# Eleven products instead of twelve for w_in from block 3 on, g as one tile, and Strassen's sums 512 wide

## The chip, the cores and the metric

The kernel runs on one NeuronCore of a Trainium2 chip. The metric is the time of one execution on the device in microseconds. Before the change it is 675.13 us, the median of three runs (674.52 to 676.1).

## The reference

A linear-attention recurrence (the delta rule) for 4 sequences, 8 heads, 768 steps and a head size of 48, in float32, feeds a two-layer network on 3072 tokens:

```python
for t in range(S):
    y[t]  = q[t] @ state
    v_old = state.T @ k_n[t]                      # k_n: k over its norm
    state = state + beta[t] * outer(k_n[t], v[t] - v_old)
x = y.transpose(...).reshape(3072, 384)           # 4*768 tokens, 8 heads * 48
h = x @ w_in                                      # w_in: 384 x 2048
g = h * clip(h + 3, 0, 6) / 6
out = g @ w_out                                   # w_out: 2048 x 384
```

The weights arrive as float64 and are converted in the kernel.

## The kernel before

**The recurrence in chunks.** The 768 steps are cut into 24 chunks of 32, and 4 sequences times 32 steps fill the 128 partitions. In chunk t the function `chain` multiplies the state with the chunk's keys and queries (`ks`, L798), forms R from v and that (L892 twice, then L898, on VectorE), multiplies R with X, a triangular inverse (`pz`, L819), copies the result to Z on ScalarE (L916), updates the state (`su`, L927 and L945), and gives the output y (`py`, `yt`), which lands transposed in `xT`. `prep` makes the chunk's normalised keys kb on GpSimd (L502), transposes keys and queries (`pt`, L516), and forms the triangular matrices (`sc`, L539 and L550); `mask` (L478) and `scaled` (L490) prepare the masks mb and the keys times beta, bkb, on GpSimd.

**The inverse.** Chunk 0 is a group by itself, and then four chunks make a group (chunks 1 to 4, 5 to 8, 9 to 12 and so on). `inverse(g)` computes X for a whole group on VectorE: a transposition (L461), 60 small elimination steps that depend on each other (L751 multiplies, L756 subtracts), a memset (L760) and a transposition into X (L465). The first chunk of the group needs X at its `pz`.

**The network in blocks.** Two chunks make a block of 256 tokens, so there are 12 blocks. The first layer of a block takes the 2048 columns of w_in in 16 pieces of 128 (`up`, L983: for each piece three products of 128x128 with 256 tokens, then Relu on ScalarE, L991, and minimum times h on VectorE, L994, into `g`). From block `UF = 5` on, `up_by_eleven` takes two pieces together: a Strassen scheme with eleven products of 128x128x128 instead of twelve, with sums of weights made once in `weight_sums` (on GpSimd, L1020, during the second layer of block `UF - 1`, some of them in w_in in place), sums of tokens made once per block in `token_sums` (VectorE, L1046), and sums inside PSUM and g: a copy on ScalarE (L1069), two additions on GpSimd (`plus_minus`, L1020), two on VectorE (L1084, L1088), a copy and a Relu on ScalarE (L1091; L1095, which writes r into the buffer of `o`) and the last step on VectorE (L1098). `T1x`, `T2x`, `T4x` lie in unused columns of `beta_tok`.

The second layer is plain for blocks 0 and 1 (`down`, L1145). From block 2 on `down_by_seven` makes seven half-size products (L1210, in two halves each) in Strassen-Winograd's way. Four sums of quarters of g are formed in place on VectorE (L1196, the function `sums`, `lo` and `hi` halves), each by four instructions that take two pieces of 128 columns. Results are copied by ScalarE (L1217), added on GpSimd or VectorE (L1220) and written out by SyncE's queue (`to_dram`, L1134).

**The order.** Every engine works in the order in which the kernel is written down; nothing is rescheduled. The first chunks follow a list written by hand (`ORDER`). From chunk 5 on a loop places, for each chunk, 15 units. In each unit it takes steps of the chain and the preparation, one unit of the network (`mlp_units`: the first layer of a block has 16, the second by seven 14 to 15) and a number of elimination steps of the next group's inverse (`fill`). How many is worked out from the room that VectorE is taken to have in this unit:

```python
USED = {"up": 0.42, "eleven": 1.0, "down": 0.8}
...
room = max(1.65 - USED[mode["of"]] - CHAIN.get(u, 0), 0.15) / mode["mean"]
due += room * left / max((GS - i) * NU - u, 1)
```

`mode["of"]` says which kind of layer runs, `mode["mean"]` is 0.72 up to the last plain first layer and 0.4 after. So `UF` and `USED` move the elimination steps too. For group 3 (chunks 9 to 12) the steps begin in chunk 7; for the later groups they begin in the second chunk of the group before.

**PSUM.** Four buffers with the tag `pm` serve ph, pt, pz, py, yt and po in turn; two with the tag `pc` serve ks, su and sc.

**The tile g.** g is allocated as eight tiles of two pieces each, [128, 2, 256], from a pool with eight buffers.

Of the kernel before, what the change touches and what calls it, by code (L numbers as in the profile page):

```python
# [9 lines left out]
FP32 = mybir.dt.float32  # L10
# [36 lines left out]
def kernel(  # L47
# [21 lines left out]
    nc = tc.nc  # L69
# [3 lines left out]
    P = B * C  # L73
# [6 lines left out]
    NFC = FF // 128  # L80
    assert NKT * 128 == DM == H * D and NFC * 128 == FF
    CB = 2
    TB = CB * P
# [121 lines left out]
    for j, value in enumerate((1.0, -1.0)):  # L205
        m = mask2[:, j, :]
        for b in range(B):
            nc.gpsimd.memset(mask2[rows(b), j, :], value)
            nc.gpsimd.affine_select(
                out=mask2[rows(b), j, :], in_=mask2[rows(b), j, :], pattern=[[1, C]],  # L210
# [96 lines left out]
    for i, n in enumerate((0, 1, 2, 3, 4, 5, 0, 1, 3, 4, 5, 0, 1, 5, 0, 1)):  # L307
        s, f = weights[i][0].shape[1:]
# [49 lines left out]
    def convert():  # L358

        needs("beta")  # L360
        for i in range(NW):
            needs(("raw", i))
            if weights[i][1].dtype != FP32:
                d = raws[i]
                hi, lo = d[:, :, :, 1], d[:, :, :, 0]
                m = spare[:, 2, WP * NKT : 2 * WP * NKT].bitcast(U32).rearrange(
                    "p (s f) -> p s f", s=d.shape[1]
                )
                mf = m.bitcast(FP32)
                nc.vector.tensor_scalar(  # L370
                    out=m, in0=hi, scalar1=0x000FFFFF, scalar2=0x00100000,
                    op0=ALU.bitwise_and, op1=ALU.bitwise_or,
                )
                yield
                nc.vector.scalar_tensor_tensor(  # L375
                    out=mf, in0=lo, scalar=2.0**-32, in1=m, op0=ALU.mult, op1=ALU.add
                )
                past.add(("seen", i, 1))
                yield
                needs(("scale", i))  # L380
                nc.vector.scalar_tensor_tensor(
                    out=weights[i][0], in0=mf, scalar=2.0**-20, in1=like(es[i % 2], i).bitcast(BF16),
                    op0=ALU.mult, op1=ALU.mult,
                )
            past.add(("w", i))
            yield
# [570 lines left out]
    gs, pos, evicts = {}, {}, []  # L957
# [13 lines left out]
    def up(blk, half_of=None):  # L971

        cols = slice(0, TB) if half_of is None else slice(half_of * P, half_of * P + P)
        name = "u" if half_of is None else "ab"[half_of]
        needs(*(("seam", blk * CB + i) for i in range(CB) if half_of in (None, i)))
        xT = xTs[blk]
        for f in range(NFC):
            needs(("w", f * 128 // WP))
            key = ("ph", blk, f, half_of)
            ring("pm", NPM, key)  # L980
            ph = psM.tile([128, TB], FP32, name="ph", tag="pm")
            for s in range(NKT):
                nc.tensor.matmul(  # L983
                    ph[:, cols], lhsT=w_in[:, s, f * 128 : (f + 1) * 128], rhs=xT[:, s, cols],
                    start=(s == 0), stop=(s == NKT - 1),
                )
            if f % 2 == 0 and not half_of:
                gs[blk, f // 2] = mlp.tile([128, 2, TB], FP32, name="g", bufs=NFC // 2)

            def first(f=f, g=gs[blk, f // 2][:, f % 2, cols], ph=ph[:, cols], key=key):  # L990
                nc.scalar.activation(out=g, in_=ph, func=ACTF.Relu, bias=half, scale=1.0 / 6.0)  # L991

                def rest():
                    nc.vector.scalar_tensor_tensor(  # L994
                        out=g, in0=g, scalar=1.0, in1=ph, op0=ALU.min, op1=ALU.mult
                    )
                    read(key)
                    if half_of is not None:
                        past.add(("g", half_of, f))

                pending[name].append(rest)

            relus[name].append(first)
            if f == NFC - 1 and not half_of == 0:
                past.add(("up", blk))
            yield

    UF = 5
    S1, S2, S4 = (sums_in[:, i] for i in range(3))

    def w_tiles(s, i):
# [37 lines left out]
    def up_by_eleven(blk):  # L1049
        needs(("sums", blk))  # L1050
        B11, T3x, B21, B22, B31, B32 = x_tiles(blk)
        phs, ready = {}, {}

        def mm(ph, n, w, x, start=False, stop=False):
            nc.tensor.matmul(  # L1055
                ph[:, n], lhsT=w, rhs=x, start=start, stop=stop, skip_group_check=True
            )

        def begin(j):
            key = ("ph", blk, "by", j)  # L1060
            ring("pm", NPM, key)
            ph = phs[j] = psM.tile([128, 4, P], FP32, name="ph", tag="pm")
            mm(ph, 0, W11[:, j], B11, start=True)
            mm(ph, 1, S1[:, j], T1x)
            mm(ph, 2, W21[:, j], T3x)
            mm(ph, 3, S2[:, j], T2x)
            gs[blk, j] = mlp.tile([128, 2, TB], FP32, name="g", bufs=NFC // 2)
            gt = gs[blk, j][:].rearrange("p i (t c) -> p (i t) c", c=P)
            nc.scalar.activation(out=gt, in_=ph[:], func=ACTF.Copy)  # L1069
            plus_minus(gt[:, 3:1:-1], gt[:, 0:2], gt[:, 3:1:-1], ALU.add)  # L1070
            plus_minus(gt[:, 0], gt[:, 0], gt[:, 2], ALU.add)

        def end(j):
            ph = phs.pop(j)
            mm(ph, 0, W12[:, j], B21)
            mm(ph, 1, S4[:, j], B22)
            mm(ph, 2, W22[:, j], T4x)
            mm(ph, 0, W13[:, j], B31)
            mm(ph, 1, W13[:, j], B32)
            mm(ph, 2, W23[:, j], B31)  # L1080
            mm(ph, 3, W23[:, j], B32, stop=True)
            g = gs[blk, j][:].rearrange("p i c -> p (i c)")
            gt = gs[blk, j][:].rearrange("p i (t c) -> p (i t) c", c=P)
            nc.vector.tensor_tensor(  # L1084
                out=gt[:, 1:3], in0=ph[:, 1:3],
                in1=gt[:, 3].unsqueeze(1).to_broadcast([128, 2, P]), op=ALU.add,
            )
            nc.vector.tensor_tensor(out=gt[:, 3], in0=ph[:, 3], in1=gt[:, 0], op=ALU.add)  # L1088

            def first():  # L1090
                nc.scalar.activation(out=gt[:, 0], in_=ph[:, 0], func=ACTF.Copy)  # L1091
                read(("ph", blk, "by", j))
                ro = mlp.tile([128, CB, DM], FP32, name="o", bufs=1)
                r = ro[:].rearrange("p c m -> p (c m)")[:, 0 : 2 * TB]
                nc.scalar.activation(out=r, in_=g, func=ACTF.Relu, bias=half, scale=1.0 / 6.0)  # L1095

                def rest():
                    nc.vector.scalar_tensor_tensor(  # L1098
                        out=g, in0=r, scalar=1.0, in1=g, op0=ALU.min, op1=ALU.mult
                    )  # L1100

                ready[j] = rest

            ready[j] = first
            if j == NPR - 1:
                past.add(("up", blk))

        def go(j):
            if j in ready:
                ready.pop(j)()  # L1110

        begin(0)
        yield
        begin(1)
        yield
        for j in range(NPR):
            end(j)
            go(j - 1)
            if j + 2 < NPR:
                yield  # L1120
                begin(j + 2)
                go(j)
                yield
            else:
                go(j)
                if j == NPR - 1:
                    go(j)
                yield
# [47 lines left out]
    def quarters():  # L1176

        for o, a, b in ((T1, B12, B11), (T2, B22, T1), (T4, T2, B21)):
            for f in range(0, HF, 2):
                nc.vector.tensor_tensor(  # L1180
                    out=o[:, f : f + 2], in0=a[:, f : f + 2], in1=b[:, f : f + 2], op=ALU.subtract
                )
                yield
# [4 lines left out]
        )  # L1188

    def down_by_seven(blk):  # L1190
        def A(f, i, j):
            return gs[blk, (f + HF * j) // 2][:, :, i * P : i * P + P]

        def sums(op, out, a, b, fs):
            for f in fs:
                nc.vector.tensor_tensor(out=A(f, *out), in0=A(f, *a), in1=A(f, *b), op=op)  # L1196

        lo, hi, A11, A12, A21, A22 = (0, 2), (4, 6), (0, 0), (0, 1), (1, 0), (1, 1)
        o = mlp.tile([128, CB, DM], FP32, name="o", bufs=1)
        u = mlp.tile([128, HM], FP32, name="u", bufs=1)[:]  # L1200
        C11, C12, C21, C22 = (o[:, c, m : m + HM] for c in range(CB) for m in (0, HM))
# [115 lines left out]
    def chained(*gens):  # L1317
        for gen in gens:
            yield from gen
# [64 lines left out]
        return norms(g, i, size(g) if g > 1 else 2 if t == 2 else 1)  # L1384

    mlp = ctx.enter_context(tc.tile_pool(name="mlp", bufs=2))
    rest = chained(convert(), quarters())
    gens.update(
        a=scales(), c=rest, w=pieces(), q=queries(), v=values(), B=betas(), k=keys(), z=settings(), s=more_settings(),
# [26 lines left out]
    with tc.manual_schedule():  # L1416
# [10 lines left out]
        fill = inverse_of(2)  # L1427
        loads = iter(())
        left = due = 0
        USED = {"up": 0.42, "eleven": 1.0, "down": 0.8}  # L1430
        CHAIN = {0: 0.45, 1: 0.75, 2: 0.75, 3: 0.4, 4: 0.4, 6: 0.5, 9: 0.8, 10: 0.6, 14: 0.2}
        for t in range(LS, N):
            g, i = group(t)
# [92 lines left out]
```

## Time and profile before

| | |
|---|---|
| time, median of three runs | 675.13 us |
| span of the profiled execution, first to last instruction | 673.6 us |
| median less span | 1.5 us |
| PE busy | 636.8 us, 95% |
| VectorE (DVE) busy | 497.2 us, 74% |
| ScalarE (ACT) busy | 271.2 us, 40% |
| GpSimd (POOL) busy | 206.4 us, 31% |
| mean granted clock of TensorE | 0.992 |

No time is given for the profiled execution beside its span; so the span is used with the 1.5 us that the median lies above it. In the profile, PE is TensorE's matmul and PEld its weight load, which overlaps; a float32 matmul of the program stands as two instructions. The slices are fortieths of the span, 16.8 us each. A group's idle time is the engine's wait in front of the group, with what ended it. The chain that ended last is followed back from the end, and where it leaves TensorE, TensorE need not have been idle: it may have had other work until just before.

In the stretch from 189 to 631 us a block takes two stages of about 25 us: the first layer of a block (with an even chunk's start in it) and its second layer (with the odd chunk's). Block 3's first layer runs from 238.27 to 265.10, block 4's from 289.79 to 316.62, and the eleven-products blocks 5, 6 and 7 from 340.93, 391.08 and 441.19. Chunk 7 starts (with `ks`) at 216.6, chunk 8 at 242.2, chunk 9 at 267.7, chunk 12 at 344.3, chunk 13 at 369.4.

### The profile page before, as it was taken

What the parts mean: (1) busy time and instruction counts of PE and PEld (TensorE: products, weight loads), DVE (VectorE), ACT (ScalarE), POOL (GpSimd) and SP (SyncE); (2) the same over time, 40 slices, a digit from 0 to 9 for tenths busy, and PEclk for the clock granted to TensorE, in tenths of its full rate; (3) what the DMA queues carried; (4) which work ended last, traced back from release to release, by engine and by line L of the source; (5) the groups of instructions that cost most, each with busy time, mean ns of one, the idle gap of its engine ahead of it and who ended that gap; (6) DMA issues with size and microseconds to landing.
All of it is one profiled execution on the core that took longest, in us unless ns stands there. A gap on an engine that the chain in (4) does not pass through costs nothing.

```text
span 673.6 us, 26871 instructions
## 1 busy us (share of the span) xinstructions
PE 636.8 (95%) x11768; PEld 578.6 (86%) x11768; DVE 497.2 (74%) x1226; ACT 271.2 (40%) x532; POOL 206.4 (31%) x320
## 2 busy tenths in 40 slices
PE   2667989999999999999999999999999999999997
PEld 2557877776688988988999999999999999999997
DVE  5978876888545678947888957988748988557354
ACT  5995777422143232232235235245244144153250
POOL 6230231102431031254155255055042141232330
PEclk9989899999999999999999999999999999999999
DMA  7995336402041030032030030020020020010000
GB/s 192 243 218 131 91 78 150 84 1 48 15 82 28 2 72 2 3 70 39 3 64 12 2 67 9 3 61 3 2 49 3 2 49 2 17 23 2 26 1 23
DMA packets 88500, 33.29 MB, mean 49 GB/s; under 512 B 80160, under 2 KB 83232, under 8 KB 88384
## 3 DMA queue, kind: packets, MB, share of 16 engines
q1 hardware_dynamic: 88128, 31.29, 20.9%
q8 instruction: 92, 1.51, 0.9%
q10 hardware_dynamic: 256, 0.30, 0.2%
q14 instruction: 24, 0.20, 0.1%
HBM read 26.84 MB, written 4.72 MB: 47 GB/s over the span
## 4 chain that ended last, share of the span: by engine, by line
PE 86%; DVE 6%; DMA 2%; ACT 2%; issue 2%; SPq 1%; POOL 0%; ACTq 0%; DVEq 0%; POOLq 0%
PE po L1210 27%; PE ph L1055 20%; PE ph L983 15%; PE po L1145 6%; PE ks L798 3%; PE pz L819 3%; PE su L927 3%; PE py L819 3%; PE sc L539 3%; PE pt L516 3%; ACT spare L348 1%; PE yt L864 1%; DVE spare L375 1%; DMA spare<-in_moe_w_in_dram 1%; DMA qb<-in_q_dram 1%
## 5 line engine op out<-in xcount | busy, mean ns | idle before, releaser
L1055 PE MATMUL ph<-xT,w_in 128*128 128x128 f32 x784 | 122.9, 278 | 0.0
L983 PE MATMUL ph<-xT,w_in 128*128 128x256 f32 (+1 forms) x576 | 114.9, 350 | 3.4 <-DVE g L994 2.1
L1210 PE MATMUL po<-w_out,g 128*128 128x192 f32 x640 | 110.6, 326 | 0.0
L983 PEld LDWEIGHTS ph<-xT,w_in 128*128 128x128 f32 x576 | 94.3, 192 | 15.3 <-DVE g L994 2.5
L1055 PEld LDWEIGHTS ph<-xT,w_in 128*128 128x128 f32 x784 | 103.9, 192 | 1.4 <-ACT KQ L524 0.2
L1210 PEld LDWEIGHTS po<-w_out,g 128*128 128x128 f32 x640 | 104.1, 190 | 0.2
L1020 POOL TENSOR_TENSOR g<-g 128x256 f32<-128x256 f32 x112 | 68.1, 610 | 83.9 <-ACT g L1069 79.5
L1210 PE MATMUL po<-spare,g 128*128 128x192 f32 x480 | 86.7, 332 | 0.0
L1210 PEld LDWEIGHTS po<-spare,g 128*128 128x128 f32 x480 | 77.2, 190 | 1.8
L991 ACT ACTIVATE g<-ph,halves 128x256 f32<-128x256 f32 (+1 forms) x96 | 41.2, 436 | 79.1 <-PE ph L983 79.1
L1220 POOL TENSOR_TENSOR o<-o,u 128x192 f32<-128x192 f32 x18 | 15.0, 835 | 172.1 <-ACT o L1217 97.4
L1196 DVE TENSOR_TENSOR g<-g 128x256 f32<-128x256 f32 x160 | 63.4, 443 | 3.4 <-PE po L1210 3.1
L1069 ACT ACTIVATE g<-ph 128x512 f32<-128x512 f32 x56 | 33.4, 596 | 79.9 <-PE ph L1055 76.7
L756 DVE TENSOR_TENSOR A<-A,pr 128x30 f32<-128x30 f32 (+9 forms) x150 | 59.0, 393 | 3.7
L751 DVE TENSOR_TENSOR pr<-A 128x30 f32<-128x30 f32 (+9 forms) x150 | 55.2, 368 | 2.7
L994 DVE SCALAR_TENSOR_TENSOR g<-g,ph 128x256 f32<-128x256 f32 (+1 forms) x96 | 35.0, 370 | 26.0 <-ACT g L991 25.7
L348 ACT ACTIVATE spare<-spare,places 128x768 uint16<-128x768 uint16 (+1 forms) x56 | 52.4, 940 | 2.0 <-DMA spare<-in_moe_w_in_dram 1.1
L1084 DVE TENSOR_TENSOR g<-ph,g 128x256 f32<-128x256 f32 x56 | 23.4, 419 | 38.1 <-PE ph L1055 24.1
L1217 ACT ACTIVATE o<-po 128x192 f32<-128x192 f32 x40 | 13.2, 330 | 82.5 <-PE po L1210 78.9
L1098 DVE SCALAR_TENSOR_TENSOR g<-o,g 128x512 f32<-128x512 f32 x56 | 40.8, 729 | 7.3 <-ACT o L1095 7.3
L1145 PE MATMUL po<-w_out,g 128*128 128x384 f32 x128 | 45.6, 493 | 0.0
L1095 ACT ACTIVATE o<-g,halves 128x512 f32<-128x512 f32 x56 | 40.5, 722 | 11.3 <-DVE g L1098 5.7
(141 smaller groups left out, 991.4 us busy)
## 6 DMA issues: line engine op xcount, KB each, us to landing
kf<-in_k_dram SPq DMA_DIRECT2D x96, 48.0 KB, 2.8
qb<-in_q_dram SPq DMA_DIRECT2D x96, 48.0 KB, 2.9
vf<-in_v_dram SPq DMA_DIRECT2D x96, 48.0 KB, 2.1
out_dram<-o SPq DMA_DIRECT2D x92, 48.0 KB, 1.6
spare<-in_moe_w_in_dram SPq DMA_DIRECT2D x4, 768.0 KB, 6.7
w_out<-in_moe_w_in_dram SPq DMA_DIRECT2D x4, 768.0 KB, 6.0
w_out<-in_moe_w_out_dram SPq DMA_DIRECT2D x4, 768.0 KB, 6.0
spare<-in_moe_w_out_dram SPq DMA_DIRECT2D x4, 768.0 KB, 4.6
```

The source lines that it names most:

```text
L348: nc.scalar.activation(out=z, in_=z if n else d.bitcast(I16)[:, :, :, 3], func=func, bias=places[:, n : n + 1], scale=scale,)
L751: nc.vector.tensor_tensor(out=pv, in0=A[:, j + 1 :, j].unsqueeze(2).to_broadcast([n, w, j]), in1=A[:, j, 0:j].unsqueeze(1).to_broadcast([n ...
L756: nc.vector.tensor_tensor(out=A[:, j + 1 :, 0:j], in0=A[:, j + 1 :, 0:j], in1=pv, op=ALU.subtract)
L983: nc.tensor.matmul(ph[:, cols], lhsT=w_in[:, s, f * 128 : (f + 1) * 128], rhs=xT[:, s, cols], start=(s == 0), stop=(s == NKT - 1),)
L991: nc.scalar.activation(out=g, in_=ph, func=ACTF.Relu, bias=half, scale=1.0 / 6.0)
L1020: nc.gpsimd.tensor_tensor(out=out, in0=a, in1=b, op=op)
L1055: nc.tensor.matmul(ph[:, n], lhsT=w, rhs=x, start=start, stop=stop, skip_group_check=True)
L1095: nc.scalar.activation(out=r, in_=g, func=ACTF.Relu, bias=half, scale=1.0 / 6.0)
L1098: nc.vector.scalar_tensor_tensor(out=g, in0=r, scalar=1.0, in1=g, op0=ALU.min, op1=ALU.mult)
L1145: nc.tensor.matmul(pos[c][:], lhsT=gs[blk, f // 2][:, f % 2, c * P : (c + 1) * P], rhs=w_out[:, f, :], start=(f == 0), stop=(f == NFC - 1),)
L1196: nc.vector.tensor_tensor(out=A(f, *out), in0=A(f, *a), in1=A(f, *b), op=op)
L1210: nc.tensor.matmul(ps[n][:], lhsT=A(f - f % 2, *a)[:, f % 2], rhs=b[:, f], start=(f == 0), stop=(f == HF - 1),)
```

## The change

`UF` becomes 3: blocks 3 and 4 also use `up_by_eleven`, and `weight_sums` runs beside block 2's second layer. g becomes one tile, `g_all`, of [128, 16, 256], allocated once for all blocks; the functions take slices of it. With that, a Strassen sum takes four pieces in one instruction (128 partitions, 4 x 128 columns) where it took two, so each of the four sums has two instructions and not four. `USED["down"]` becomes 0.7.

```diff
-            if f % 2 == 0 and not half_of:
-                gs[blk, f // 2] = mlp.tile([128, 2, TB], FP32, name="g", bufs=NFC // 2)
+            gs[blk, f // 2] = g_all[:, f - f % 2 : f - f % 2 + 2]
...
-    UF = 5
+    UF = 3
...
-            gs[blk, j] = mlp.tile([128, 2, TB], FP32, name="g", bufs=NFC // 2)
-            gt = gs[blk, j][:].rearrange("p i (t c) -> p (i t) c", c=P)
+            gs[blk, j] = g_all[:, 2 * j : 2 * j + 2]
+            gt = gs[blk, j].rearrange("p i (t c) -> p (i t) c", c=P)
...
-        def A(f, i, j):
-            return gs[blk, (f + HF * j) // 2][:, :, i * P : i * P + P]
-
-        def sums(op, out, a, b, fs):
-            for f in fs:
-                nc.vector.tensor_tensor(out=A(f, *out), in0=A(f, *a), in1=A(f, *b), op=op)
-
-        lo, hi, A11, A12, A21, A22 = (0, 2), (4, 6), (0, 0), (0, 1), (1, 0), (1, 1)
+        def A(f, i, j, n=2):
+            return g_all[:, f + HF * j : f + HF * j + n, i * P : i * P + P]
+
+        def sums(op, out, a, b, f):
+            nc.vector.tensor_tensor(out=A(f, *out, 4), in0=A(f, *a, 4), in1=A(f, *b, 4), op=op)
+
+        lo, hi, A11, A12, A21, A22 = 0, 4, (0, 0), (0, 1), (1, 0), (1, 1)
...
+    g_all = mlp.tile([128, NFC, TB], FP32, name="g", bufs=1)
...
-        USED = {"up": 0.42, "eleven": 1.0, "down": 0.8}
+        USED = {"up": 0.42, "eleven": 1.0, "down": 0.7}
```

## Prediction

> **What bounds the kernel now.** I read the page first (busy shares, slices), then the table by stage, then the chain that ended last, then VectorE's timeline at two seams.
>
> ```profile
> PE 636.8 (95%) x11768; PEld 578.6 (86%) x11768; DVE 497.2 (74%) x1226; ACT 271.2 (40%) x532; POOL 206.4 (31%) x320
> PE   2667989999999999999999999999999999999997
> DVE  5978876888545678947888957988748988557354
> ```
>
> TensorE is full from about 105 us to the end, so past the start only two things change the time: TensorE work, and moments when TensorE waits. The stages show what a block's first layer costs (columns: length, busy time and instructions of PE, PEld, DVE, ACT, POOL, then clock, DMA share, GB/s):
>
> ```profile
> 238.27:265.10 26.83, 26.83 (x429) 23.03 (x428) 23.78 (x60) 9.56 (x20) 6.45 (x9) 1.00 0.23 46
> 289.79:316.62 26.83, 26.83 (x429) 23.04 (x428) 16.34 (x40) 9.56 (x20) 15.47 (x23) 1.00 0.36 69
> 340.93:366.77 25.84, 25.84 (x509) 25.15 (x508) 22.98 (x52) 12.93 (x26) 14.43 (x23) 1.00 0.24 49
> 391.08:416.88 25.80, 25.80 (x508) 25.11 (x508) 16.54 (x39) 12.93 (x26) 13.58 (x23) 1.00 0.24 49
> ```
>
> The first two rows are blocks 3 and 4 by plain products, the others blocks 5 and 6 by eleven; the recurrence's pieces between the products are the same. The third thing to see is a seam (start, length, what), where the inverse for chunks 9 to 12 ends and `pz` of chunk 9 needs it:
>
> ```profile
> 267.70 1.08 PE ks L798 x64
> ...
> 273.24 1.99 DVE X L465
> 275.23 0.14 issue
> 275.37 0.88 PE pz L819 x63
> ```
>
> From the start of `ks`, TensorE has other work for 7.37 us (1.08 + 1.51 + 0.44 + 1.30 + 0.44 + 2.60 in the chain), to 275.07. X ends at 275.23: TensorE loses 0.3 us. Here VectorE has no slack at all, and the change loads VectorE just ahead of this point. The fourth view is VectorE's timeline behind an eleven-products block (block 5), where TensorE's `ks` starts at 369.37:
>
> ```profile
> 368.77 0.68 DVE L1098 SCALAR_TENSOR_TENSOR g<-o,g 128x512 f32<-128x512 f32 x1
> 370.30 0.69 DVE L1098 SCALAR_TENSOR_TENSOR g<-o,g 128x512 f32<-128x512 f32 x1 [0.85 <-ACT o L1095]
> ...
> 372.49 1.99 DVE L465 STREAM_TRANSPOSE X<-A 128x1024 f32<-128x1024 f32 x1
> 374.32 0.67 DVE L892 SCALAR_TENSOR_TENSOR R<-ks,parity,vf 128x192 f32<-128x192 f32 x2
> ```
>
> The block's last VectorE step ends at 370.99, 1.62 us after `ks` has started. Behind a plain block VectorE is ahead instead: at 268.73 R only waits for `ks`.
>
> **Step 1, TensorE.** Blocks 3 and 4 change kind: 96 matmul instructions of 256 columns become 176 of 128. In stage time 26.83 becomes 25.80 to 25.84 (26.14 in block 7, the worst): 1.0 us saved a block, bounds 0.7 and 1.03, so -2.0 for two, between -1.4 and -2.06. All of it is on the path.
>
> A rule speaks against it. The Trainium skill, "TensorE: Matmul & The Clock Gate", section "Back-to-back issue gap", gives about 81 ns sustained for each load-and-multiply pair of 128 columns and 131 of 512, so narrow products pay for their loads; a straight line gives an estimated 98 ns at 256, and a block would go from 96 x 98 = 9.4 to 176 x 81 = 14.3 us, 4.9 longer. The rows of this float32 kernel differ: the last block's 176 take 19.71 us, 112 ns each, and sixteen plain groups run at 1.30 us for 6, 216 ns each, so twice the columns cost nearly twice.
>
> **Step 2, other engines in blocks 3 and 4.** ScalarE goes from 9.56 to 12.93 of 26 us and GpSimd gets 16 more `plus_minus`, 8 x (0.75 + 0.47) = 9.8 us, to about 14 of 26: the rows of blocks 5 and 6 hide the same, so nothing. The weight sums (16 of 0.73 us, 12 us) move from 293 to 328 us on GpSimd to around block 2, where GpSimd is busy 3.9 of 24 and 4.1 of 25 us. Behind them are kb, mb and bkb, used later; the in-place one waits for the first layer's reads (1.9 us here), which GpSimd can afford. Nothing, but 1 to 2 us if kb came late. `r` in the buffer of `o` brings a new wait of L1095 for the previous block's output DMAs; behind L1095 are L1098 and R on VectorE, and `pz` on TensorE. In blocks 5 and 6 L1095 starts 6.41 us into the block; block 2's output has landed at 243.24 against 244.7, block 3's at 295.56 against 296.2. Hidden by 1.4 and 0.6 us; where the cover was gone (block 8, ScalarE waits 1.74) TensorE lost 0.64.
>
> **Step 3, VectorE's bill.** A plain block has 16 L994 of 0.39 = 6.2 us; an eleven block 8 x (0.39 + 0.29 + 0.66) = 10.7, and token sums of 1.9: +6.4 us a block. The Strassen sums: two 256 wide take 0.74 in the timeline, a 512-wide one is not in the trace. L1098, same shape and also two tiles read, repeats every 0.60 when alone; so 0.60 to 0.74. I take 0.63, near L1098, which saves 0.1 on each of 80, 0.9 us a block. In steady blocks that is slack, worth nothing. The first of each pair waits a little longer for TensorE's reads, 0.2 us, in an engine that is idle there.
>
> **Step 4, where it is late.** I counted the elimination steps (L751 and L756, "fills") in the built program's order between R's of neighbouring chunks. Chunks 7, 8, 9 have 21, 30, 8 before X and 26, 26, 6 after; `USED` of 0.7 puts more into 7. With durations from the trace chunk 8 holds 24.4 us of VectorE work for 20.9, in 25 us of TensorE. Block 5 (chunk 12) is the measure: there 14 fills, 5.3 us, stand before the last L1098, in chunk 8 there are 18 larger ones, 7.5 us. Of the 2.2 more, two VectorE gaps of chunk 12 (0.39 at 351.9, 0.52 at 355.8) take 0.9: the last L1098 ends 1.3 later than 1.62. Bounds: 0, if the gaps of 0.80 and 0.85 absorb as well, and 2.2.
>
> Behind it, in order, to X: fills of 168, 150, 130, 108 columns, two of each (0.73 + 0.70 + 0.62 + 0.57), R 0.64, one sum 0.63, two fills of 84 (0.55), L898 0.53, fills of 58 and 30 (0.51 + 0.42), L760 0.12, X 1.99: 8.0 us, start to start as between 264 and 275 us. Low 7.6; high 9.0 if GpSimd slows them: the L756 of 130 columns takes 0.29 at 267.7 and 0.71 at 364.6 beside GpSimd's work.
>
> X ends 1.62 + 1.3 + 8.0 = 10.9 us after `ks` starts; with 0.14 for the release 11.06, against 7.37: TensorE stalls 3.7, bounds 2.0 and 5.6. The 0.3 there now is inside, so +3.4 (+1.7 to +5.3). VectorE recovers in chunk 9 (19 us of work for 25 plus the stall); from group 4 on X stands a chunk earlier, at the end of chunks 12, 16 and 20, as now.
>
> **The sum.** -2.0 + 3.4 = +1.4 us on the span of 673.6, so 675.0, and 1.5 around it (median 675.13 less span): 676.5, with the bounds 674.7 to 679.0. About 0.2% (1.35 us) is what a measurement of this kernel can tell from no change, so the forecast is slower by just that.
>
> **The rivals.**
> - *The gain stays.* VectorE catches up: the last L1098 is no later than 1.62, the eight fills fit into its idle places (2.6 us of gaps in chunk 12), X about 1 us late at most. For it: before block 3, R need not lag 2.8 us as in chunk 12, since chunk 7 has 21.8 us of work. Against: that lag is wiped out at the second L1084 anyway, which waits for TensorE, and from 356 us on chunk 12 has no gap but the last. It decides if X ends under 9.4 us after `ks`: then the stall is below 2.3 and the time not above 675.1. With X in time -2.0 - 0.3: 672.8; with 1 us late 673.8. I put it at 673.4.
> - *VectorE's lateness reaches TensorE inside block 3.* Four `pm` buffers serve ph, pt, pz, py, yt; a late L1088 delays L1091, which frees ph. And L898 gets a fill in front of it, where `pz` leaves 0.8 us in chunk 12 (L898 ends at 350.63, `pz` starts at 351.40). For it: the waits list PEld `pz` behind ACT L1091 once, 0.8 us. Against: no PE wait on it in seven blocks. If both bite in blocks 3 and 4, 1 us each: 678.5.
> - *Fewer products, no gain.* If weight or token sums arrive after block 3's start, TensorE waits 1 to 2 us there: 678. Block 5's token sums ended at 340.84 against 340.93; chunk 7 has one fill more in front of them. Small.
>
> **How the numbers follow.** Sum as worked out 0.6 (of it 0.33 within 1.35 us, 0.26 above, 0.01 below); gain stays 0.2 (0.17 faster, 0.03 same); lateness inside the block 0.15 and late sums 0.05, slower. Faster 0.18, same 0.36, slower 0.46. The range leaves out about 0.1 of the gain's low end and 0.1 of the two slow rivals' and the sum's high end: 673.4 to 678.8.
>
> **What would show it.** Stages of blocks 3 and 4 near 25.8 us of TensorE; one new gap of 2 to 5.6 us in front of `pz` near 273, released by X L465; L465 10 to 12 us after `ks`; a chain that leaves TensorE there for VectorE over most of a chunk; sums at 0.60 to 0.74; ScalarE's wait for out_dram still below 2 us. A gap under 1 us there, or a TensorE stage above 26.5, would make it wrong.

## The result, and the profile after

The changed kernel takes 681.63 us (median of 4 executions, 679.03 to 681.82), beside 675.24 us for the kernel before (4 executions, 674.52 to 676.1): ratio 1.0075, 95% interval 1.0054 to 1.0097. It is slower, as forecast, but by 6.4 us and not by 1.4, and above the range of 673.4 to 678.8. Some executions of both kernels and of the variants below ran disturbed, at a lower granted clock throughout: the medians leave them out, and of the two profiles that fell into one (`after_again`, clock 0.846, and `before_pad64`, 0.937) only the places and lengths of gaps are used. Lines behind 983 move up by one or two: L1098 of before is L1097 now, L1196 is L1194, L1210 is L1208.

The page of the changed kernel, with the lines that answer to those of before (busy shares, then tenths in 40 slices):

```profile
span 679.9 us, 27216 instructions
...
PE 641.6 (94%) x11928; PEld 588.5 (87%) x11928; DVE 505.1 (74%) x1170; ACT 281.0 (41%) x548; POOL 226.9 (33%) x352
...
PE   2677988999999999899999999999999999999997
...
DVE  5987875889536889857988857989757988557353
...
PEclk9567898999999999899999999999999999999999
```

The kernel before has this line of granted clocks:

```profile
PEclk9989899999999999999999999999999999999999
```

In PEclk two things are new. Slices 1 to 3 stand at 5, 6 and 7: TensorE ran part of the start at half its clock. And near slice 16 (272 us on) an 8 stands, in PE's line and in PEclk's, at the seam that Step 4 was about. Block 3's first layer, a half-clock stretch just behind it, and block 4's first layer show this by stage (columns as in the table of before):

```profile
242.12:269.21 27.09, 25.86 (x509) 24.98 (x508) 25.10 (x57) 12.77 (x25) 15.00 (x22) 1.00 0.23 47
281.70:285.10 3.40, 3.27 (x130) 3.02 (x131) 2.88 (x7) 0.49 (x1) 0.00 (x0) 0.50 0.02 5
297.56:323.36 25.80, 25.80 (x509) 25.11 (x508) 16.80 (x40) 12.94 (x26) 13.61 (x23) 1.00 0.36 71
```

The third row is Step 1's forecast: 25.80 us for 26.83, so 1.03 saved. In the first row PE is busy for 25.86 of 27.09, so 1.23 us of block 3 are a wait. The timeline of TensorE names it, and the one at the seam (a wait and its releaser stand in brackets):

```profile
264.80 0.55 PE L864 MATMUL yt<-ident,y 128*128 128x128 f32 x3 [1.23 <-DVE y L854]
...
271.90 1.15 PE L798 MATMUL ks<-state,KQ 64*64 64x48 f32 x64
...
281.83 1.50 PE L819 MATMUL pz<-R,X 32*32 32x48 f32 x64 [2.50 <-DVE X L465]
```

`pz` also takes 1.50 us for the 0.88 of before: it stands in the second row of the stage table, a stretch of 3.4 us at a granted clock of 0.50. VectorE's side, in its timeline, is the chain of Step 4:

```profile
273.30 0.69 DVE L1097 SCALAR_TENSOR_TENSOR g<-o,g 128x512 f32<-128x512 f32 x1 [0.85 <-ACT o L1094]
...
277.18 0.68 DVE L1194 TENSOR_TENSOR g<-g 128x512 f32<-128x512 f32 x1
...
279.75 1.93 DVE L465 STREAM_TRANSPOSE X<-A 128x1024 f32<-128x1024 f32 x1
```

I compare the profiles chunk by chunk, from one `ks` to the next. Chunk 4 starts at 121.10 us before and at 124.96 after: +3.86, in a stretch where both kernels have the same instructions. From there to the end the changed kernel takes 2.43 us longer (554.98 for 552.55): two blocks at -1.03, +1.23 for y, +2.50 for X less the 0.31 of before, about +1.4 for the half clock (an estimate from the longer `pz`, `sc` and products of that stretch), -0.7 for a stall that stood only in the profile of before (in its block 8), and 0.4 in small pieces. So behind chunk 4 this profile comes near the forecast of +1.4 with a clock loss on top. The larger part of its loss lies ahead of chunk 4, where the forecast had nothing. The profile doesn't explain 6.4 us, nor why the same kernel took 683.7 and 683.5 in later measurements.

### The profile page after: what moved, and what is told of

The parts are those of the page before. It is cut to its first block, busy times and chain, and to the rows that moved or that the text cites. A ratio compares the mean times of both kernels' runs of the same rounds, so it can differ in the third digit from the quotient of the medians.

```text
span 679.9 us, 27216 instructions
## 1 busy us (share of the span) xinstructions
PE 641.6 (94%) x11928; PEld 588.5 (87%) x11928; DVE 505.1 (74%) x1170; ACT 281.0 (41%) x548; POOL 226.9 (33%) x352
## 4 chain that ended last, share of the span: by engine, by line
PE 84%; DMA 5%; DVE 4%; ACT 2%; SPq 2%; issue 2%; POOL 0%; ACTq 0%; DVEq 0%; POOLq 0%
PE po L1208 26%; PE ph L1054 25%; PE ph L983 10%; PE po L1144 6%; PE ks L798 4%; PE pz L819 3%; PE py L819 3%; PE su L927 3%; PE sc L539 2%; DMA w_out<-in_moe_w_in_dram 2%; PE pt L516 2%; DMA qb<-in_q_dram 1%; DMA spare<-in_moe_w_in_dram 1%; ACT spare L348 1%; PE yt L864 1%
## 5 line engine op out<-in xcount | busy, mean ns | idle before, releaser
L1054 PE MATMUL ph<-xT,w_in 128*128 128x128 f32 x1008 | 158.5, 278 | 0.1
L1019 POOL TENSOR_TENSOR g<-g 128x256 f32<-128x256 f32 (+1 forms) x144 | 88.7, 617 | 107.5 <-ACT g L1068 101.9
L1208 PE MATMUL po<-w_out,g 128*128 128x192 f32 x640 | 110.6, 326 | 0.0
L1208 PEld LDWEIGHTS po<-w_out,g 128*128 128x128 f32 x640 | 103.9, 190 | 0.1
L1208 PE MATMUL po<-spare,g 128*128 128x192 f32 x480 | 87.1, 333 | 0.0
L1068 ACT ACTIVATE g<-ph 128x512 f32<-128x512 f32 x72 | 43.0, 597 | 105.4 <-PE ph L1054 102.2
L1208 PEld LDWEIGHTS po<-spare,g 128*128 128x128 f32 x480 | 77.6, 191 | 1.9 <-issue 0.2
L983 PE MATMUL ph<-xT,w_in 128*128 128x128 f32 (+1 forms) x384 | 73.9, 347 | 1.8 <-ACT spare L348 1.8
L983 PEld LDWEIGHTS ph<-xT,w_in 128*128 128x128 f32 x384 | 62.0, 204 | 9.0 <-ACT spare L348 1.9
L1083 DVE TENSOR_TENSOR g<-ph,g 128x256 f32<-128x256 f32 x72 | 30.1, 419 | 46.5 <-PE ph L1054 30.3
L1097 DVE SCALAR_TENSOR_TENSOR g<-o,g 128x512 f32<-128x512 f32 x72 | 52.8, 733 | 8.1 <-ACT o L1094 8.1
L1194 DVE TENSOR_TENSOR g<-g 128x512 f32<-128x512 f32 x80 | 55.3, 712 | 3.0 <-PE po L1208 2.9
L1094 ACT ACTIVATE o<-g,halves 128x512 f32<-128x512 f32 x72 | 52.0, 723 | 11.6 <-DVE g L1097 7.5
L1054 PE MATMUL ph<-beta_tok,sums_in 128*128 128x128 f32 x288 | 55.7, 275 | 0.0
L524 ACT ACTIVATE KQ<-pt 128x512 f32<-128x512 f32 x48 | 28.0, 593 | 40.3 <-PE pt L516 39.7
```

The source lines that it names most:

```text
L983: nc.tensor.matmul(ph[:, cols], lhsT=w_in[:, s, f * 128 : (f + 1) * 128], rhs=xT[:, s, cols], start=(s == 0), stop=(s == NKT - 1),)
L1019: nc.gpsimd.tensor_tensor(out=out, in0=a, in1=b, op=op)
L1054: nc.tensor.matmul(ph[:, n], lhsT=w, rhs=x, start=start, stop=stop, skip_group_check=True)
L1097: nc.vector.scalar_tensor_tensor(out=g, in0=r, scalar=1.0, in1=g, op0=ALU.min, op1=ALU.mult)
L1194: nc.vector.tensor_tensor(out=A(f, *out, 4), in0=A(f, *a, 4), in1=A(f, *b, 4), op=op)
L1208: nc.tensor.matmul(ps[n][:], lhsT=A(f - f % 2, *a)[:, f % 2], rhs=b[:, f], start=(f == 0), stop=(f == HF - 1),)
```

## The experiments

Each kernel was timed against the kernel before on the same chip. The paddings below change TensorE's instruction count alone; TensorE's order is otherwise untouched, and so are the other engines.

**Round 1: VectorE's lateness.** The changed kernel again; with `UF = 4`; the g tile and the 512-wide sums without the earlier eleven products; and with the inverse brought forward.

`after_again`, no edit:

> The changed kernel once more. In its first profile 3.9 us of the 6.3 lay before 190 us, where both programs are the same instruction by instruction. Theory V (VectorE late in block 3; the start is this execution's chance): block 3's two stages 3.9 us longer than before, block 4's 1.0 shorter, the start sometimes late and sometimes not, as in the kernel before; time 677.5 to 678.5 where the start is alike, ratio about 1.004. Theory S (the start belongs to the changed kernel): 681.6 again, start 3 to 4 us late in nearly every execution, ratio 1.0095.

683.68 us, ratio 1.0123 (1.0087 to 1.0158). So 681.6 was no outlier. Its profile has a wait that the first profile lacked: three gaps in `sc`, in chunks 8, 12 and 16, of 1.62, 0.99 and 0.88 us, with no releaser. The line below is the third, from TensorE's timeline:

```profile
502.04 0.31 PE L539 MATMUL sc<-KQ 64*32 64x64 f32 x6 [0.88 <-issue]
```

`uf4`:

```diff
-    UF = 3
+    UF = 4
```

> The change with UF = 4: block 3 by plain products, block 4 by eleven. V: block 4's first stage 1.0 us shorter, no wait for y in block 3, the wait for X in front of pz of chunk 9 at most 0.3 us: 673.5 to 674.5 with a start like before's, ratio 0.998. S: the same behind a late start, 677.5, ratio 1.004.

677.59 us, ratio 1.0022 (1.0 to 1.0045). One block less by eleven products, and most of the loss is gone. The ratio lies between V's 0.998 and S's 1.004, so neither theory was met. In its profile no wait for X or y is left (25, 30 and 4 elimination steps in chunks 7, 8, 9); L983 waits 1.03 us for VectorE's L993 once. The one eleven block's saving of 1.0 is spent on that.

`sums_only`, the changed kernel with the two numbers of before:

```diff
-    UF = 3
+    UF = 5
...
-        USED = {"up": 0.42, "eleven": 1.0, "down": 0.7}
+        USED = {"up": 0.42, "eleven": 1.0, "down": 0.8}
```

> Only g as one tile and the sums 512 wide (UF = 5 and USED of 0.8 as before). V: 80 sums for 160, at about 0.65 us, in VectorE's slack: 0 to -0.4 us, 675.0, ratio 0.9995. S, if it is g's tile that makes the start late: 679, ratio 1.006; if not, as V.

676.34 us, ratio 0.9995 (0.9967 to 1.0022). g as one tile and the wider sums are worth nothing that can be measured, as Step 3 had it ("slack"). The whole loss belongs to `UF` and to the elimination steps that `UF` and `USED` move; the 0.7 was not tried by itself.

`early_inverse`, which places 38, 20 and 0 elimination steps in chunks 7, 8 and 9 (changed kernel 26, 26, 6), so that X ends in chunk 8:

```diff
-                due = min(due, 2.6)
+                due = min(due, 5.0 if t == 7 else 2.6)
```

> The whole change, and in chunk 7 the cap of 2.6 on the elimination steps of a unit is 5.0: 38 steps in chunk 7, 20 in chunk 8 with X at its end, none in chunk 9 (26, 26 and 6 in the changed kernel). V: no wait for X, the wait for y in block 3 under 0.3 us, no half-clock stretch behind them: 5 us less than the changed kernel, 672.5 to 673.5 with a start like before's, ratio 0.997. S: 676.5, ratio 1.002. If steps in chunk 7 make VectorE late there instead, a wait of 1 to 2 us appears in front of pz of chunk 8 (about 252 us).

682.91 us, ratio 1.0097 (1.0068 to 1.0127). TensorE's waits from 125 us on:

```profile
PE sc L539 <- issue: 4.6, 3, 1.7
PE yt L864 <- DVE y L854: 1.6, 1, 1.6
PE ph L1054 <- ACT KQ L524: 0.6, 1, 0.6
```

The wait for X is gone, so Step 4's mechanism is real and can be taken away. The load moves to chunk 7, where `yt` now waits for y. But the time hardly moves, where V had forecast 5 us less, and the largest row is the one without a releaser ("issue").

**What these gaps are.** They come at the same place in different runs. I numbered TensorE's instructions in each trace (matmuls, weight loads, waits). The gaps of `sc` stood at 9665, 13505 and 17345 in both `after_again` and `early_inverse`: 3840 apart, 15 times 256, and 193 over a multiple of 256. The trace has a queue of kind "instruction" with 94 packets of 16,384 bytes (92 in the kernel before), for 24,043 TensorE instructions (23,714): one packet for 256. Each takes 0.9 to 1.6 us. And `pz` with `sc` are 256 instructions in 1.6 us (0.88 + 0.81 and their overlap), the fastest stretch of the kernel. That gave theory P: where a block of 256 begins late in `sc` (I call this place a border), the block in front of it has been used up within about 2 us, and the next is not there yet. Four chunks with eleven-products blocks have 3832 instructions, 8 less than 15 such blocks, so the place recurs every four chunks, each time 8 instructions further on in `sc`; `UF = 3` shifts it by 329 instructions against the kernel before. The Trainium skill, "Runtime: NRT & Kernel Launch", section "Instruction fetch mechanics", says that instructions come in 16 KiB blocks of 256, and that crossing a border is mostly hidden; the rows agree with the first, and with the second at most borders, but not at those late in `sc`.

**Round 2: paddings in chunk 0.** 128 more TensorE instructions in the changed kernel, 64 in the kernel before, by issuing some `sc` matmuls of chunk 0 twice; and 128 with two amounts of advance of the inverse.

```diff
-        for p in range(NP):
+        for p in [*range(NP), *([0] * 4 if t == 0 else [])]:      # * 2 in the kernel before
```

`after_pad128`:

> The changed kernel; only the sc matmuls of chunk 0 are partly issued a second time with the same values, 32 matmuls more, which is 128 TensorE instructions (0.7 us at a time when TensorE waits for loads anyway). Everything behind them stands 128 instructions later in TensorE's program. Theory P (TensorE's instructions are loaded in blocks of 256; where a block begins just before the 256 short instructions of pz and sc, the next one is not there in time): the gaps of 0.9 to 1.7 us in sc of chunks 8, 12, 16, seen in the repeated run of the changed kernel and in the run with the earlier inverse, are gone, the waits for y (1.2) and X (2.5) stay: 679 to 680 us. Theory V (only VectorE's lateness): same time as the changed kernel, 681.6 to 684.

684.28 us, ratio 1.0122 (1.0078 to 1.0167): no faster. The gaps are gone from chunks 8, 12 and 16, as P said, but new ones stand in chunks 10 and 14 (1.84 and 1.52 us), again at 193. Neighbouring chunks lie 55 to 77 instructions apart in phase, two chunks about 128, so a padding of 128 hands the border to another chunk. I had not worked that out.

`before_pad64`:

> The kernel before, with 16 more sc matmuls in chunk 0 (64 TensorE instructions, 0.4 us where TensorE waits for loads). Theory P: the block border that lies in the middle of pz in the eleven-products chunks 12, 16, 20 moves to the last instructions of sc, and up to three gaps of 0.9 to 1.7 us without a releaser appear there, each perhaps with a half-clock stretch behind it: 678 to 681 us. Theory V: no change, 675 to 676.6 us.

681.78 us, ratio 1.0089 (1.0057 to 1.012). The kernel before becomes 5.8 us slower by 64 instructions (6.7 by the median of all eleven executions), with gaps of 2.05 and 1.28 us at the places forecast, chunks 12 and 16.

`early_pad128` and `early34_pad128` (cap 5.0 and 3.4 in chunk 7, and 128 of padding):

> The changed kernel with the inverse for chunks 9 to 12 finished in chunk 8 (as in the run before with this edit, 682.9) and the 128 instructions of padding. P: the three gaps of 1.4 to 1.7 us in sc go with their clock losses, about -6 us: 676 to 678; the wait of yt for y in chunk 7 (1.5) stays, the wait for X is gone. V: 683 as without the padding.

> The padding of 128, and a milder advance of the inverse: elimination steps 33, 23, 2 in chunks 7, 8, 9 where the changed kernel has 26, 26, 6 and the run with the earlier inverse 38, 20, 0. P with V: X ends about 1.6 us earlier than in the changed kernel, so its wait is 0.5 to 1 us for 2.5, and chunk 7 delays yt less than 1.5 us; no gaps in sc: 675 to 677 us. V alone, without P: 679 to 682.

682.49 us (1.0083, 1.0048 to 1.0118) and 683.83 us (1.0112, 1.0066 to 1.0158). Both have the two gaps of the padding (1.89 and 1.88; 1.62 and 1.36), so both expectations fail for the same reason as `after_pad128`. The milder advance did what it should at X and y: 0.99 and 0.60 us for 2.50 and 1.23.

**Round 3: a padding of 24**, which puts no border between the 101st and 126th instruction of `sc`.

```diff
-                for e in range(2):
+                for e in ((0, 1, 0, 1) if t == p == 0 and b < 3 else range(2)):
```

> The changed kernel with 24 more TensorE instructions in chunk 0 (6 sc matmuls of that chunk issued twice). In all ten gaps seen in sc so far the instruction that came late stands at the same remainder, 193 of 256, in TensorE's stream, between the 101st and the 126th of the 128 of sc. With 24 the borders move to the 77th, 85th and 93rd in chunks 8, 12 and 16, and to just behind sc (the 132nd and later) in chunks 9, 13, 17, so that 50 slower instructions of a product lie inside each block. Theory P: no gap in sc above 0.5 us; the waits for y (1.2) and X (2.5) and the half-clock stretch behind X stay: 678 to 680. Theory V: as without, 681.6 to 684.

> The kernel before with the same 24 instructions. Its borders at the 106th and 113th instruction of sc in chunks 11 and 14 (no gap seen there in its one profile) go to the 82nd and 89th. P: 0 to 1 us faster than before, if unprofiled runs had a gap there at times: 675 to 676. V: 676.

> The milder advance of the inverse (elimination steps 33, 23, 2 in chunks 7, 8, 9) with the 24 instructions of padding. Waits as with the padding of 128: 0.6 for the first layer in chunk 7, 0.6 for y, 1.0 for X (2.2 in all, for 3.7 in the changed kernel) and no gap in sc. P and V together: -2.0 for the products, +2.2 - 0.3 for the waits, no half-clock stretch, so the level of before, 675 to 677. If it stays at 680 or more, neither P nor V holds the whole of the loss.

`after_pad24` 684.05 us (1.0123, 1.0095 to 1.0152), `before_pad24` 678.01 us (1.0044, 1.0027 to 1.0061), `early34_pad24` 684.0 us (1.0115, 1.0087 to 1.0142). All gaps in `sc` went, as expected; the times did not follow. One gap moved to the product behind `sc` in chunk 9 (1.15 and 1.33 us), which I had taken to be safe. And the kernel before lost 2.6 us by the padding itself with no gap in its profile behind 125 us: a padding in chunk 0 also moves the borders of the start, so it can't tell the start from the gaps. Between the two padded kernels 6.0 us remain, of which the profiles show 4.5 from chunk 4 on.

**Round 4: the same by paddings at 115 us**, in `sc` of chunk 6, so that the start stays the kernel's own; and the changed kernel a third time.

```diff
-                for e in range(2):
+                for e in (0, 1, 0, 1)[: 4 if t == 6 and p < 2 else 2]:                     # before, 64
+                for e in (0, 1, 0, 1)[: (4, 4, 3, 2)[b] if t == 6 and p == 0 else 2]:      # after, 20
```

`before_late64`:

> The kernel before with 64 more TensorE instructions at 115 us (0.4 us), start untouched. P: gaps of 1 to 2 us at the end of sc in chunks 12, 16 and perhaps 20, as with the padding of 64 in chunk 0: 679 to 681. C: the 6.7 us of that earlier padding came from the start, so 676 to 677 here.

681.77 us, ratio 1.0079 (1.0053 to 1.0105), so +5.5 us (3.6 to 7.1) for 0.4 us of instructions. TensorE's timeline at chunk 12, and its waits from 125 us on:

```profile
355.55 0.81 PE L539 MATMUL sc<-KQ 64*32 64x64 f32 x59
358.43 0.43 PE L539 MATMUL sc<-KQ 64*32 64x64 f32 x5 [2.06 <-issue]
```

```profile
PE sc L539 <- issue: 3.2, 2, 2.1
PE pz L819 <- DVE X L465: 0.3, 1, 0.3
```

The stretch behind this gap, as a window:

```profile
358.00:361.40 3.40, 2.97 (x17) 2.81 (x18) 0.76 (x2) 0.51 (x2) 0.00 (x0) 0.56 0.18 35
```

The reader is to see a gap without releaser that cuts `sc` after 59 of 64 matmuls, and behind it 3.4 us at a mean clock of 0.56. Chunk 12 takes 28.91 us for 25.03. Two of the forecast gaps are there, and the start was not touched: the phase of the instruction blocks alone costs the kernel before nearly what the change cost it (5.5 us beside 6.4 to 7.3).

`after_third`:

> The changed kernel as it is, once more on the chip of the other three. P: its profile shows gaps of 0.9 to 1.7 us in sc of chunks 8, 12, 16 (3 to 5 us with clock losses), 682 to 684. C: no such gaps, and chunk 4 starts at 125 us or later for 121.1 in the kernel before.

683.47 us, ratio 1.0092 (1.0055 to 1.0128). Its waits from 125 us on, and chunk 8 in the timeline:

```profile
PE sc L539 <- issue: 3.2, 2, 1.9
PE pz L819 <- DVE X L465: 2.4, 1, 2.4
```

```profile
252.50 0.74 PE L539 MATMUL sc<-KQ 64*32 64x64 f32 x50
255.10 0.34 PE L539 MATMUL sc<-KQ 64*32 64x64 f32 x14 [1.86 <-issue]
```

Gaps in chunks 8 and 16 of the three forecast. The wait for y is gone: TensorE was late already. From chunk 4 on this execution takes 558.40 us, 5.85 more than before, where the first profile had 2.43.

`after_late20`:

> The changed kernel with 20 more TensorE instructions at 115 us (5 sc matmuls of chunk 6 issued twice, 0.13 us), so the first 115 us are the changed kernel's own, which the paddings in chunk 0 were not. The late instructions move from the 101st, 109th and 117th of sc (chunks 8, 12, 16) to the 81st, 89th and 97th, and in chunks 9, 13, 17 to the 136th and later, which is behind sc. Theory P (the gaps where a new block of 256 instructions begins make up what the first profile of the changed kernel did not show): 679 to 681, 3 below the unpadded kernel on the same chip. Theory C (the start, or something else that the stages behind chunk 4 do not show, is later in this kernel): within 1.5 us of the unpadded one, 682 to 684.

681.39 us, ratio 1.0068 (1.004 to 1.0096): 2.1 below the unpadded kernel, in the direction of P, but the intervals overlap, and the time lies between what P and C had forecast. No gap in `sc`; the one behind it in chunk 9 stays, in the waits from 125 us on:

```profile
PE pz L819 <- DVE X L465: 2.5, 1, 2.5
PE po L1208 <- issue: 1.3, 2, 1.1
PE yt L864 <- DVE y L854: 1.2, 1, 1.2
PE ph L1054 <- ACT KQ L524: 0.4, 1, 0.4
```

`early34_late20`, the same with the cap of 3.4 in chunk 7:

> The milder advance of the inverse with the late padding of 20. P with V: 2.2 us of waits for 3.7, no half-clock stretch and no gap in sc: 676 to 678. C: 680 or more.

680.13 us, ratio 1.006 (1.0031 to 1.0089). VectorE's waits are 1.6 us (X 1.0, y 0.6) for 3.7, and the time is 1.3 lower, again within overlapping intervals. Two gaps of 0.75 and 0.68 us at block borders remain. It misses P's expectation by 2 us, just meets C's "680 or more", and is still slower than before. No version beat the kernel before.

**The 24 gaps.** In the 15 kernels run and the first two profiles, 24 gaps of over 0.3 us without a releaser stand between 125 us and the last product, 0.40 to 2.06 us long: 18 in `sc`, the others in `py` or in the products shortly behind such a burst. All 24 begin at the remainder 193. Every gap at another remainder has an engine as its releaser (X, y, KQ, g, R, o). The packets of the instruction queue show what the 24 wait for. They come in order, so each border has its packet. All 24 gaps end 1.21 to 1.51 us after the border's own packet has landed. At the other 1213 borders behind 125 us the packet landed at least 1.32 us before its instructions began, 5.6 us in the median. So TensorE was waiting for its instructions. A packet starts 0.7 us (median) after TensorE has crossed the border in front; with 0.9 us to land and 1.2 more to the first instruction that is some 2.8 us (an estimate from these figures), too late where a block is used up in 2 us.

## Why the prediction was right or wrong

**Step 1 held**: 25.80 us for 26.83 in block 4, at its value of 1.0.

**Step 2 held**: no wait for the weight sums, and none for the buffer of `o` on TensorE's side. L1094's 0.85 us in front of the last L1097 is the one of block 5 before.

**Step 3** priced the 512-wide sum at 0.63 between 0.60 and 0.74; the median is 0.68, 0.60 start to start where the next step follows at once. It decided nothing, as `sums_only` shows.

**Step 4 had the mechanism and the place right, and the split wrong.** X ended 9.79 us after `ks`, not 10.9: the last L1097 was done 2.1 after `ks` (forecast 2.9), the work behind it took 7.7 (forecast 8.0). TensorE's other work covered 7.43 (forecast 7.37). So `pz` waited 2.50, in the bounds of 2.0 to 5.6. The missing 1.2 had been paid already: the second rival, lateness inside the block, came true at another place than named, `yt` waiting 1.23 for y behind four elimination steps. Together 3.73, beside 3.7 forecast for X alone; the agreement of the sums is partly luck. `early_inverse` shows that the wait for X comes from the steps' placing, and also that VectorE's load then delays y in chunk 7: it had no slack before block 3 to catch up in, against the first rival.

**What failed is the sum: it had no term for TensorE itself.** The prediction took the path to consist of TensorE's work and of waits that an engine releases ("past the start only two things change the time"). A third was missing: waits for TensorE's own instructions, which the sum put at nothing. The changed kernel has 329 TensorE instructions more, and from block 3 on the 256-instruction borders fall late in `sc` of chunks 8, 12 and 16. In `after_third` that cost gaps of 1.86 and 1.37 us and the clock behind them, 3.4 us from chunk 4 on beyond the first profile. That this is a cause and not a companion is shown by `before_late64`: with no other change the kernel before loses 5.5 us. For the changed kernel the reverse is less clear: with the borders moved out of `sc` (`after_late20`) it gained 2.1 us, within overlapping intervals.

**A second missing term is the clock behind a wait.** A wait of 2.5 us was followed by 3.4 us at a granted clock of 0.50, worth about 1.4 us more, in the first profile; in `after_late20` no such stretch followed the same wait. The traces show what decides. In each of them the granted clock changes only on a grid of steps of 3.41 us. Between 125 and 640 us, in all 17 profiles, TensorE was idle for 1.70 to 2.46 us of a step six times, and each time the next step ran at 0.50. Of two steps with 1.62 and 1.66 us of idle time the first was followed by one, and no step with less. The wait of the first profile lay with 2.39 us in one step; that of `after_late20` was cut by a step's end into 1.66 and 0.83. Where the grid lies is chance, but the term goes one way only.

**What stays open.** Gaps, waits and clock give 2.4 to 5.9 us from chunk 4 on, and the medians differ by 6.4 to 7.3. About 1 us remains also for `before_late64` (5.5 for 4.6 from chunk 4 on). The start could hold it: in the first profile 3.86 of the 6.3 us arose ahead of chunk 4, where the sum had no term. Chunk 4 began at 121.5 to 127.2 us in five profiles of kernels with `UF = 3` and unpadded start, at 121.1 to 124.5 in four of the others. The ranges overlap and each profile is one draw, so neither a later start nor its absence is shown. The half clock alone does not make a start late: up to chunk 4 the mean clock was 0.82 in the first profile, but 0.96 both in `before` (121.10 us) and in `after_third` (124.11 us). Nor is it shown why the gaps are missing in one execution of a kernel and there in another. In the first profile the packets of the three places had landed 1.86 to 2.04 us ahead; what made them start earlier there stays open. A border late in `sc` is not enough by itself either: the kernel before has them at the 106th and 113th instruction of `sc` in chunks 11 and 15, and in its profile their packets had landed 4.3 us ahead, without a gap.

## What to carry to other kernels

When a stage that runs TensorE without a pause is rewritten with more and smaller instructions, add a term for where the 256-instruction borders fall: look for the places where a few hundred tiny instructions run at some 6 ns each (0.81 us for the 128 of `sc`), and for gaps in the trace that nothing releases. Before blaming the edit for a loss of one per cent, add a few dozen harmless instructions to both kernels at a point that leaves the start alone; if the kernel before then loses as much, the arithmetic need not be the cause. And one profile is one draw: the first one here had none of the gaps in `sc`.

## What the runs showed of the hardware that was not expected

- TensorE can run out of instructions: with `pz` and `sc` 256 of them go in 1.6 us, a block of 16,384 bytes takes 0.9 to 1.6 us to land, and 24 gaps of 0.40 to 2.06 us all began at the same remainder of 256 and ended 1.21 to 1.51 us after the block's landing.
- A short wait can halve the clock. Behind 2.50 us of waiting the granted clock was 0.50 for one step of 3.41 us, and so it was behind 2.06 us (the window above has a mean of 0.56 because it begins before the step). From 125 us on, 1.70 us of idle time within one step were enough each time, and less than 1.62 us never. The Trainium skill, "TensorE: Matmul & The Clock Gate", section "Part 1: The HAM clock gate (the "warmup" mystery)", names an idle window of about 3.4 us as the condition; here shorter waits were enough.
- With the same instructions in the first 115 us, chunk 4 began between 121.1 and 127.2 us in nine profiles, a spread as large as the effect under study.
